# W1 loaded into the memory of W2 and of hT's second buffer, with a new list of orders and engines

## The chip, the cores and the metric

The kernel runs on one core of a Trainium2 chip. The time is device microseconds of one execution, from the first to the last instruction with what the launch adds around them; the median of three runs of the kernel before is 260.54 us (260.16 to 260.61). Engines are named as in the profile: PE (TensorE, matmul), DVE (VectorE), ACT (ScalarE), POOL (GpSimd) and SP (SyncE, which only issues transfers).

## The reference

Nyström attention on q, k and v of shape 8 x 8 x 576 x 64 (batch, heads, sequence, head size), then a feed-forward block on the result, seen as 8 x 576 x 512:

```python
q_lm, k_lm = means of q and k over 32 segments of 18 rows
A, Bm, C = sm(q, k_lm), sm(q_lm, k_lm), sm(q_lm, k)
Z = Bm.T / (norm1(Bm) * norminf(Bm) + 1e-6)
for _ in range(6):
    Z = 2 * Z - Z @ Bm @ Z
x = A @ Z @ C @ v                       # heads put side by side: 576 x 512 per batch
xn = (x - mean(x)) / sqrt(var(x) + 1e-6) * g_ln
out = x + relu(xn @ w_ch1) @ w_ch2      # 512 -> 2048 -> 512
```

## The kernel before, in words

The work is cut into 1571 named operations, each with the engines that may do it and the buffers it uses. A list at the top of the file (`ORDER`, lines 19 to 105) gives the order in which they are emitted and the engine of each, so `28G` is operation 28 on POOL, `95S` operation 95 issued by SP. Every engine works off its own operations strictly in that order; where one waits, all behind it on that engine wait too. A buffer's slot is given out at its first use and comes back after its last, in the order of the list.

Eight batches are computed. Batch 0 is prepared alone, batch 1 alone, then 2 and 3, 4 and 5, 6 and 7 in pairs. For a batch, the stages are:

- loads of q, k and v. For batch 0 SP loads fp32 into the staging buffers `stg` (six slots), and an operation `cast_...` turns each into fp16 (`nat_q`, `nat_k`, `natv`). For the other batches POOL loads q and k with the conversion in the transfer, and SP loads v into two buffers `vs`.
- for batch 0: transposes on PE (`turns_k0` and so on), their copies (`turned_...`, to `xT_k`, `xT_q`), segment sums (`sums_...`), `klm` and `qbd`, then `psb_0`, `expb_0`, `softmax_0` (line 366), `gram_a_0`, `gram_b_0`, `scaled_0` and six iterations `step_0_i` (PE) and `next_0_i` (DVE, line 425), then `product_0` with v, `rcv_0`, `cv_00`, `cv_01`, `zt`, `zc`, and the copies `ztc`, `zsum`, `zcbd`. `ea` holds the exponentials of A; `ln`, `inv` (ACT) and `norm` normalize it.
- `rows` and `x`: the attention's output in blocks of 128 rows, `measure` its mean and variance.
- `psm_bf`, `m16_bf`: W1 multiplied by the batch's small matrix, in four quarters f of 512 columns; for batches 0 and 1 the column mean of W1 (`less_f`, from `less_mean_fc` on PE) is added in `m16`.
- `psh`, `relu`: the hidden rows, 16 chunks of 128 for a batch, evicted by ACT or DVE into `hT` (two buffers, `hT0` and `hT1`, by the batch's parity).
- `pso`, or from batch 2 on a scheme with seven products of halves (`ps7a`, `ps7c`, `ps7e`, with sums `mix` of quarters of W2), then `done`/`add7` into x and the stores.

Weights: g is loaded as `g_rows`, turned by PE (`turn_g`) and written to `g_sb` by DVE. W1 (512 x 2048, fp32, 4 MB) comes in eight pieces of 512 KB, `load_w1_i`, piece i holding quarter f = i // 2 and half of the 512 rows. In the kernel before each goes into a slot of `stg`, which q, k and v of batch 0 have used first, so the load waits for a cast to free one. Two operations `scale_w1_ic` per piece multiply by g and write fp16 to `w1_16` (line 357 on POOL and DVE, line 203 on ACT). W2 is loaded by POOL in four pieces with conversion into `w2_16`.

`warm_i` are matmuls on zeros, 24 of 160 columns in one and four of 128 in each of 14 others, which stand in PE's order while the first data come in.

In the kernel before, SP's order begins k01, k00, q00, q01, v00, v01, g, then W1's pieces 2, 3, 1, 0, 4, 5, 6, v10, piece 7, v11. POOL's begins with the constants, `cast_k01`, `load_q10`, `load_k10`, `cast_v00`, the first scalings.

Of the kernel before, what the change touches and what calls it, by code (L numbers as in the profile page):

```python
# [16 lines left out]
P = 128  # L17

ORDER = """
0G 20P 23P 4S 12P 14P 24P 17P 11P 2S 1S 3S 6S 7S 10P 21P 28G 38P 25A 26D 34P 39D 40P 29P 30A 31P 27D  # L20
37P 32P 42D 41D 18P 33D 43P 65P 44A 45D 66A 61P 67P 46P 47P 250G 48D 22P 19P 15P 62A 68A 69A 71D
245G 49P 50D 63P 35P 13P 79G 80D 51P 52D 64A 36A 81P 70D 53P 72P 73A 5S 95S 54D 8P 9D 105A 106G 55P
56D 57P 74P 82D 260P 83D 58D 16P 84D 96S 59P 75A 76A 60D 85P 251D 86D 89P 90D 87P 88D 126P 261A 262D
108G 77G 94S 103G 93S 97S 101G 91D 92D 78D 107A 102G 127P 128P 129P 130A 167P 141P 142A 252P 253A
145P 169D 104A 168D 98S 254D 149P 150D 147P 148A 172P 173A 176P 247P 177A 248A 259D 255D 174P 175A
246D 256P 257A 146A 170P 171D 109G 110G 121P 122P 123P 111G 124P 268P 156P 258D 151D 249D 267P 112A
125A 275A 269A 270A 271A 157D 277A 158D 131P 132P 133P 134P 178P 163P 278D 279D 117G 273A 433G 274A
99S 113G 135A 180D 263S 164A 159P 280P 281D 160A 165P 166A 114G 264A 100S 115G 116G 265S 118G 136P
137P 266G 161P 179D 429G 119G 138P 139P 162D 282P 283D 140A 181P 182A 183P 284P 276D 285A 143P 187P
184D 286P 144A 188A 272D 152D 185P 186A 287D 297P 298D 299D 189P 191D 190D 288P 289A 294P 290P 295A  # L30
201P 202P 296A 300P 301A 291D 292P 293A 120G 455G 212P 213P 435G 436G 437G 310P 438G 445G 302A 303G
308P 309A 214P 330P 434D 444D 312D 311D 313D 332D 192P 193A 153D 154D 198P 199A 155A 441D 430D 439D
431D 331D 442D 440D 432D 443D 234P 556D 215P 304P 235P 236P 305A 306A 196P 446G 447G 203P 204P 194P
195A 237P 238P 205P 206P 451G 197A 307G 314P 315A 337P 339P 448G 449D 822G 338A 555D 239P 240P 241P
322P 207P 208P 574D 565D 569G 450D 340A 323A 216P 242D 209D 210S 217P 324D 341P 343D 223P 335P 244S
336A 342D 333P 463D 218P 219P 577G 452D 220D 344P 352P 353D 467G 468G 469G 470G 334A 826G 348P 345A
349A 346P 347A 457G 318P 319A 224P 316P 317A 225P 226P 227P 481P 458G 465D 459G 460G 482A 350P 454D
354D 357P 471D 464D 472D 351A 453D 363P 228P 229P 364D 358A 361P 230P 362A 461D 462D 365D 493P 494A
359P 368P 360A 483P 495P 355P 325D 326D 505A 369A 356A 231D 233A 200G 374P 375P 366P 367A 370P 371A
573G 506D 456D 507P 508P 509D 320P 321D 385P 484P 486A 487A 489A 510P 834D 511D 466D 491A 386P 387P  # L40
485A 388P 211S 512P 376P 473S 474G 490A 377P 496P 498A 501A 499A 497A 513D 514P 327D 488D 492D 328D
396P 397P 475S 476G 566G 828G 829G 830G 831G 572G 477S 478G 838G 839G 844G 564G 568G 503A 378P 379P
380P 515D 823D 502A 221S 504D 372P 516P 479S 480A 500D 517D 836D 528P 529P 530D 531D 398P 399P 373A
381P 522P 518P 389P 329A 866S 382D 418P 519D 824D 559D 520P 521D 523A 532P 419P 420P 524A 533A 534A
558D 550P 551D 552D 553D 548P 549A 421P 422P 423P 536P 424P 425P 848G 535G 832D 833D 554D 232S 867A
537A 538A 539G 560D 525P 527A 400P 401P 557D 426D 427S 605P 526A 606A 840G 841G 594P 595A 561D 540P
541A 390P 391P 611P 612A 837D 596D 827D 392P 393D 825D 850G 851G 852G 563D 603P 604A 853G 562D 859D
842D 860G 861G 843D 579P 613P 614A 407P 580A 601P 602A 609P 610A 1217G 585P 408P 845D 599P 409P 607P
600A 410P 411P 586A 597P 608A 542A 543G 856D 615P 598A 576G 626P 616A 412P 413P 581P 627A 402P 862G
394S 582A 570G 567D 617D 589D 835D 863G 858D 590D 618P 619A 634P 635A 643P 583P 584A 620P 621A 624P  # L50
414P 571G 874P 625A 622P 623A 628P 629A 644P 544P 847D 857D 545A 846D 591D 546A 875D 403P 632P 872S
633A 645P 630P 647P 592D 631A 646P 415D 877P 648P 649P 650P 864D 865D 854D 404D 855D 1191G 886P 638D
637G 641G 663P 664P 665P 639D 640D 662G 428S 417S 406S 661D 593A 882A 884A 879A 880A 883A 652D 878A
651D 657D 887A 889P 892A 896A 658D 666P 668D 894A 895A 849D 667D 653P 654P 711P 722P 712A 723A 891A
890A 655P 656P 547G 575G 675P 676P 677P 728P 729A 678P 695P 696A 1192D 713D 716P 881D 1194D 717A
724P 725A 876P 888P 1213G 660D 587P 870S 714P 416S 659D 871G 873G 384S 1229G 642G 1230G 1231G 726P
898A 715A 679D 682D 669P 897D 727A 588A 730P 222S 1232G 899D 900P 901P 731A 718P 732P 902D 743P 719D
578G 903P 904D 670P 720P 734A 733A 721D 744A 671P 672P 673D 699P 700A 893D 739P 636G 1203D 1239S
701P 905P 243S 741P 906D 740A 751P 674D 742A 703P 752A 907P 735P 736A 737P 383S 868S 681S 680S 683S
738A 702D 908D 909P 1219G 1195G 1220G 1221G 685P 704D 697P 698A 915P 917A 916A 910D 911P 1222G 759P  # L60
760P 749P 811P 925P 750A 761P 885D 869G 921P 926A 927A 753G 922P 1225D 755G 912D 913P 705D 706D 745P
# [1202 lines left out]
```

## Time and profile before

| | |
|---|---|
| runs | 260.16, 260.54, 260.61 us |
| profiled execution, span from first to last instruction | 258.5 us (2.0 below the median of the runs; its own time with the launch is not recorded) |
| PE busy | 249.9 us, 97% |
| DVE busy | 212.3 us, 82% |
| ACT busy | 163.9 us, 63% |
| POOL busy | 177.5 us, 69% |
| granted TensorE clock | 1.00 throughout |
| moved by DMA | 36.32 MB |

In the profile the first number of a row of a timeline is its start and the second its length, in us from the start of the span; "x8" counts the instructions put together, and the part in brackets is the time that the engine stood idle before it and what ended it. "PE busy" counts a matmul to its modelled end and so overstates how full PE is where matmuls are few. In the chain of waits each piece was released by the one before it. In the rows by stretch, the columns are the stretch, its length, the busy time of PE, weight loads, DVE, ACT and POOL with counts, the granted clock, the DMA share and GB/s. A line number is often that of a helper (L193 matmul, L200 copy, L203 ACT's function, L207 two-tensor operation, L210 scalar-tensor-tensor), so rows are told apart by the tiles.

### The profile page before, as it was taken

To read this page: it belongs to the slowest core of one execution; us is meant where nothing else is said; L and a number is where in the kernel's file an instruction comes from. 1 tells how busy PE (TensorE), PEld (TensorE's weight loads), DVE (VectorE), ACT (ScalarE), POOL (GpSimd) and SP (SyncE) were. 2 spreads that over 40 slices of the span, in tenths; PEclk is the share of its full clock that TensorE was granted. 3 is DMA by queue.
4 is the path that set the end of the run, shared out by engine and by line. 5 is a ranking of instruction groups with operands and counts; after the bars stand their busy time and mean duration, and the time that the engine had idled before them with its cause. 6 is when DMAs were issued, how large, how long until landed. Compare 5 with 4: busy or idle time off the path is not lost.

```text
span 258.5 us, 8351 instructions
## 1 busy us (share of the span) xinstructions
PE 249.9 (97%) x3499; PEld 179.8 (70%) x3499; DVE 212.3 (82%) x472; ACT 163.9 (63%) x304; POOL 177.5 (69%) x180
## 2 busy tenths in 40 slices
PE   7898999999999999999999999999999999999993
PEld 7766465556554557777766787777867787788981
DVE  1669899999999989997998869898547999878661
ACT  1588886747766999778756997868666245644000
POOL 8324899689794789699999995782078505966600
PEclk9999999999999999999999999999999999999999
DMA  6999999999749176949704832500130100510356
GB/s 234 367 269 338 374 210 208 207 235 244 227 127 178 29 164 87 221 89 286 140 4 121 231 93 61 127 3 3 41 85 0 44 20 9 115 23 20 82 121 184
DMA packets 23277, 36.32 MB, mean 140 GB/s; under 512 B 2116, under 2 KB 11592, under 8 KB 23240
## 3 DMA queue, kind: packets, MB, share of 16 engines
q1 hardware_dynamic: 12456, 23.37, 29.6%
q0 software_dynamic: 9504, 10.36, 25.1%
q10 hardware_dynamic: 1280, 2.07, 3.1%
q8 instruction: 27, 0.44, 0.7%
q14 instruction: 10, 0.08, 0.1%
HBM read 36.70 MB, written 9.44 MB: 178 GB/s over the span
## 4 chain that ended last, share of the span: by engine, by line
PE 85%; DMA 7%; ACT 3%; DVE 2%; issue 1%; SPq 1%; ACTq 0%; DVEq 0%
PE psh L193 23%; PE ps7a L193 16%; PE pso L193 15%; PE ps7c L193 8%; DMA w1s<-in_moe_w_ch_dram 5%; PE ps7e L193 4%; PE psm L193 3%; PE psy L193 3%; DMA stg_q<-in_q_dram 3%; PE it L193 2%; PE pscv L193 2%; PE psd L193 1%; PE psec L193 1%; PE psea L193 1%; PE pso_74a L193 1%
## 5 line engine op out<-in xcount | busy, mean ns | idle before, releaser
L203 ACT ACTIVATE hT<-psh 128x576 f16<-128x576 f32 x106 | 65.8, 650 | 30.4 <-PE psh L193 28.6
L193 PEld LDWEIGHTS <-hT 128*128 128x128 f16 x688 | 64.6, 98 | 22.6 <-issue 3.1
L193 PE MATMUL psh<-ea,m 128*128 128x288 f16 x512 | 78.2, 286 | 0.1
L193 PEld LDWEIGHTS <-m 128*128 128x128 f16 x512 | 48.9, 98 | 15.6 <-issue 1.3
L193 PE MATMUL pso<-w,hT 128*128 128x512 f16 x176 | 45.5, 380 | 0.0
L207 POOL TENSOR_TENSOR mix<-hT 128x1024 f16<-128x1024 f16 x8 | 17.0, 2125 | 27.4 <-ACT hT L203 27.4
L210 DVE SCALAR_TENSOR_TENSOR x<-ps7a,rstd,x 128x256 f32<-128x256 f32 x48 | 21.3, 477 | 6.7 <-PE ps7a L193 4.9
L193 PE MATMUL ps7a<-mix,hT 128*128 128x256 f16 x192 | 25.9, 273 | 0.0
L1068 DVE TENSOR_SCALAR hT<-psh 128x576 f16<-128x576 f32 x22 | 16.4, 753 | 10.1 <-PE psh L193 9.9
L997 DVE BATCH_NORM_STATS2 six<-x 128x6 f32<-128x512 f32 x36 | 24.2, 673 | 0.0
L207 POOL TENSOR_TENSOR ea<-ea,lns 128x576 f16<-128x576 f16 (+1 forms) x14 | 17.7, 1261 | 7.2 <-ACT lns L203 4.0
L200 ACT CAST m<-psm 128x512 f16<-128x512 f32 (+1 forms) x25 | 19.1, 793 | 4.5 <-PE psm L193 3.4
L200 ACT COPY x<-psy 128x512 f32<-128x512 f32 (+1 forms) x29 | 16.8, 587 | 7.6 <-PE psy L193 7.2
L193 PEld LDWEIGHTS <-mix 128*128 128x128 f16 x192 | 18.2, 98 | 4.3 <-issue 1.5
L207 POOL TENSOR_TENSOR mix<-mix,hT 128x1024 f16<-128x1024 f16 x8 | 16.9, 2124 | 6.2 <-DVE mix L207 5.8
L207 POOL TENSOR_TENSOR hT<-hT 128x1024 f16<-128x1024 f16 x9 | 19.1, 2123 | 0.2
L207 POOL TENSOR_TENSOR hT<-hT,mix 128x1024 f16<-128x1024 f16 x7 | 15.1, 2166 | 4.4 <-PE ps7e L193 2.5
L214 DVE TENSOR_REDUCE part<-xT_k 128x32 f16<-128x576 f16 x24 | 17.1, 737 | 0.0
L207 POOL TENSOR_TENSOR asum_q<-asum_q 128x256 f32<-128x256 f32 (+1 forms) x24 | 15.1, 628 | 1.5
L203 ACT ACTIVATE ec<-psec 128x256 f16<-128x256 f32 (+1 forms) x42 | 12.4, 428 | 5.3 <-PE psec L193 5.3
L193 PE MATMUL psy<-zcbd,ea 128*128 128x256 f16 x80 | 14.8, 273 | 0.2 <-ACT x L200 0.2
L200 POOL CAST natv<-stg_v 128x1152 f16<-128x1152 f32 (+1 forms) x12 | 13.8, 1163 | 1.4 <-DMA stg_v<-in_v_dram 1.3
(174 smaller groups left out, 471.2 us busy)
## 6 DMA issues: line engine op xcount, KB each, us to landing
out_dram<-x SPq DMA_DIRECT2D x55, 128.0 KB, 2.7
stg_v<-in_v_dram SPq DMA_DIRECT2D x10, 576.0 KB, 5.1
w1s<-in_moe_w_ch_dram SPq DMA_DIRECT2D x8, 512.0 KB, 11.6
nat_q<-in_q_dram POOLq DMA_DIRECT2D x7, 576.0 KB, 8.7
nat_k<-in_k_dram POOLq DMA_DIRECT2D x7, 576.0 KB, 7.5
w<-in_moe_w_ch_dram POOLq DMA_DIRECT2D x4, 512.0 KB, 8.5
out_dram<-x ACTq DMA_DIRECT2D x15, 128.0 KB, 2.4
stg_v<-in_v_dram SPq DMA_DIRECT2D x6, 288.0 KB, 4.5
```

The lines of the kernel that those rows point to most:

```text
L193: keep(nc.tensor.matmul(o, l, r, start=start, stop=stop, tile_position=(rb, cb), skip_group_check=(skip or cb != 0)))
L200: keep(nc.scalar.copy(o, i) if e == "A" else ENGINES[e].tensor_copy(out=o, in_=i))
L203: keep(nc.scalar.activation(*args, **kw))
L207: keep(ENGINES[e].tensor_tensor(out=o, in0=a, in1=b, op=f))
L210: keep(ENGINES[e].scalar_tensor_tensor(out=o, in0=a, scalar=s, in1=b, op0=f0, op1=f1))
L214: keep(nc.vector.tensor_reduce(out=o, in_=i, axis=axis, op=f))
L997: keep(nc.vector.bn_stats(out=T(f"six_{j}")[:], in_=T(f"x_{j}")[:]))
L1068: keep(nc.vector.tensor_scalar(out=o, in0=T(psh)[:, :, 0:HS], scalar1=0.0, scalar2=None, op0=ALU.max))
```

## The change

W1's pieces get no buffers of their own. Pieces 0 to 3 are loaded into the memory of `w2_16` (a quarter each, seen as fp32), pieces 4 to 7 into the second buffer of `hT`, which is then taken from the start of the program. A W1 load needs no staging slot any more. A load of W2 now has to wait until the scalings that read the W1 piece in the same quarter are done, and the first writes to the second hT buffer until the scalings of pieces 4 to 7 are.

```diff
     def def_weights():
+        if hT(1) not in kinds:
+            buf(hT(1), "hT1", [P, MCH, S + 64], FP16)
+
+        def place_of(i):
+            f, half = divmod(i, 2)
+            if f < 2:
+                return w2_16[:, ts(i, 4), :].rearrange("p m d -> p (m d)").bitcast(FP32).rearrange(
+                    "p (c d) -> p c d", c=2)
+            return T(hT(1))[:].rearrange("p m t -> p (m t)")[:, ts(i - 4, 4 * DM)].bitcast(FP32).rearrange(
+                "p (c d) -> p c d", c=2)
+
+        def held(i):
+            return () if i < 4 else (hT(1),)
+
         for i in range(8):
-            n = f"w1s_{i}"
-            buf(n, "stg", [P, 2, DM], FP32)
             f, half = divmod(i, 2)
-            op(f"load_w1_{i}", "S", (n,),
-               lambda e, n=n, f=f, half=half: dma(
-                   e, T(n)[:], w1_src[:, 2 * half:2 * half + 2, ts(f, DM)]))
+            op(f"load_w1_{i}", "S", held(i),
+               lambda e, i=i, f=f, half=half: dma(e, place_of(i), w1_src[:, 2 * half:2 * half + 2, ts(f, DM)]))
...
-                def scale(e, n=n, f=f, c=c, kk=kk):
-                    o, src = w1_16[:, kk, ts(f, DM)], T(n)[:, c, :]
+                def scale(e, i=i, f=f, c=c, kk=kk):
+                    o, src = w1_16[:, kk, ts(f, DM)], place_of(i)[:, c, :]
...
-                op(f"scale_w1_{i}{c}", "GAD", (n,), scale)
+                op(f"scale_w1_{i}{c}", "GAD", held(i), scale)
```

The list of orders is new for its first 727 operations, up to the middle of the preparation of batches 4 and 5; the other 844 are the same. The operations and their numbers are the same, and 46 of them change their engine. What the new list does, by engine, where it differs early:

- SP: k00, k01, q00, g, q01, v01, W1's pieces 2, then v00, then pieces 3, 0, 4, 1, 5, 6, v11, 7, v10.
- PE: twelve `warm` operations (before: nine) stand ahead of the first transposes, the other three between `turns_k0` and `turns_k1` (before: six spread to the end of the iterations). `turn_g` follows `turns_k1`. `product_0` stands behind `step_0_4`, the first two `less_mean` of quarter 1 ahead of it; `product_10` of batch 1 and its last steps stand behind the first `pso` of batch 0.
- DVE: `cast_k00`, `turned_k0`, `cast_q00`, `turned_k1`, `turned_q0`, `qbd`, `turned_q1`, `softmax_0`, `scaled_0`, `g`, then the iterations with `cast_v00` behind the fourth. New on DVE are `cast_q00`, `turned_q0`, `turned_q1` (from ACT), `cast_v00` and `scale_w1_10` (from POOL), `norm_10_0` (from POOL); gone from it are `cast_q01`, `klm`, three `relu` of batch 0 and three `next_1_i` (to ACT), three `norm` of batch 0 and `cast_v01` (to POOL).
- ACT: `cast_q01`, `klm`, `expb_0`, and so on; it scales parts of pieces 2, 3, 0, 5 and 7 (before 2, 3, 1 and 5), with `less_0` ahead of its scaling of piece 5 (before: behind it); `cast_v10` goes to POOL.
- POOL: the constants, `load_q10`, `cast_k01`, `cast_v01`, `load_k10`, four `norm` of batch 0 among the scalings; `load_w2_0` behind the scaling of piece 5, then `load_w2_1` and `load_q20` behind those of pieces 6 and 7 (before: `load_w2_0`, `load_q20`, those scalings, `load_w2_1`).

```diff
-0G 20P 23P 4S 12P 14P 24P 17P 11P 2S 1S 3S 6S 7S 10P 21P 28G 38P 25A 26D 34P 39D 40P 29P 30A 31P 27D
...
+2S 0G 24P 22P 19P 17P 250G 4S 16P 20P 21P 15P 14P 10P 28G 1S 26D 5S 3S 18P 23P 32P 27A 33D 7S 13P
...
```

165 lines of the change are left out of this document (82 added, 83 removed).

## The prediction

> **What bounds the kernel now.** I read the page first, then the chain of waits, the DMA view of the first 35 us, the busy time by stretch, and last the timeline of the start, row by row. The page and two of the stretches:
>
> ```profile
> span 258.5 us, 8351 instructions
> PE 85%; DMA 7%; ACT 3%; DVE 2%; issue 1%; SPq 1%; ACTq 0%; DVEq 0%
> 24.00:30.00 6.00, 5.71 (x96) 3.47 (x93) 5.01 (x11) 5.01 (x15) 4.82 (x7) 1.00 1.05 396
> 40.00:50.00 10.00, 10.00 (x90) 5.48 (x89) 9.84 (x21) 6.62 (x15) 8.76 (x12) 1.00 1.23 208
> ```
>
> From about 40 us on TensorE (the first column after the length) has no gap left, and the chain that ended last is 85% TensorE. The matmuls are the same before and after, so the end moves by what the change does to the moment at which TensorE is full, and by little else. The rest of the chain lies in the first 40 us; these are its pieces that matter:
>
> ```profile
> 15.84 11.95 DMA w1s<-in_moe_w_ch_dram
> 27.81 0.73 ACT w L203
> 28.89 0.12 ACT less L200
> 29.04 1.42 DVE m L210 x2
> 30.91 0.61 PE psh L193 x4
> ...
> 36.51 0.56 ACT hT L203
> ...
> 37.12 0.75 PE pscv L193 x34
> ...
> 38.28 0.44 DVE cv L207
> 39.53 0.86 PE pso L193 x4
> ```
>
> The sixth piece of W1 is issued at 15.84, lands 11.95 us later, ScalarE scales it at 27.81, and only then comes the column mean (less) of the first quarter of W1, the m tiles and at 30.91 the hidden rows. It looks as if W1 were late because it waited for staging buffers. The DMA view of the first 35 us (40 slices of 0.875 us) says otherwise:
>
> ```profile
> GB/s 0 0 84 276 398 408 400 411 406 392 398 390 359 283 292 249 231 257 279 290 281 302 266 276 280 300 377 406 421 389 377 404 398 390 389 367 273 222 215 202
> w1s<-in_moe_w_ch_dram SPq DMA_DIRECT2D x8, 512.0 KB, 11.6
> ```
>
> ```profile
> 6.12 1.37 POOL L223 DMA_DIRECT2D nat_q<-in_q_dram  x1
> ```
>
> From 3.5 us there is no hole. Where the figure falls to 231 to 302 the loads issued by POOL are in flight, which turn fp32 into fp16 on the way and are counted by the smaller side. A 512 KB piece at 400 GB/s is 1.3 us of transfer, and takes 11.6 us to land: it stands in a queue behind others. The W1 pieces were waiting in the DMA queue, not for its doors.
>
> **The change, part by part.** *The loads of W1.* The eight issues stay on SP, lose their wait for a freed staging buffer, and so enter the queue up to 10 us earlier. They cost nothing more, and gain nothing in sum, since the engines that carry them are full. What counts is the order of the bytes. Before: k, q, v of batch 0, then pieces 2, 3, 1, 0, 4, 5, 6, v, 7, v. After: v01 ahead of piece 2, v00 behind it, then 3, 0, 4, 1, 5, 6, v, 7, v. So piece 5 is still the sixth (lands at 27.8 as now), piece 1, which the first quarter needs, falls from third to fifth place (two pieces, 2.6 us), and v00 lands after piece 2 and not before it. POOL issues its load of q of batch 1 (now at 6.12) ahead of its first cast; if that brings its bytes forward by its own 1.4 us, SP's queue loses half of the bandwidth for as long, and piece 3 lands up to 1.4 us later. Bounds for piece 3: 0 and +1.4; I take +0.7.
>
> *The start.* These rows carry the first chain:
>
> ```profile
> 1.40 6.26 PE L193 MATMUL idle<-zeros 128*128 128x128 f16 x56 [1.40 <-DVE zeros L252]
> 13.11 0.84 PE L193 MATMUL idle<-zeros 128*128 128x128 f16 x12
> 8.20 0.76 DVE L200 COPY xT_k<-pst_k 128x1152 f16<-128x1152 f16 x1 [1.03 <-PE pst_k L197]
> 9.42 0.76 DVE L200 CAST nat_q<-stg_q 128x1152 f16<-128x1152 f32 x1 [0.47 <-DMA stg_q<-in_q_dram]
> 10.79 0.42 DVE L207 TENSOR_TENSOR qbd<-pss_q,mask 128x256 f16<-128x256 f32 x1 [0.41 <-PE pss_q L193]
> 11.89 0.21 DVE L214 TENSOR_REDUCE rsum<-it 128x2 f32<-128x64 f32 x1
> 13.70 0.22 DVE L207 TENSOR_TENSOR st<-it,cinv 128x64 f16<-128x64 f32 x1
> 17.48 0.29 DVE L210 SCALAR_TENSOR_TENSOR st<-st,it 128x128 f16<-128x128 f16 x1
> 18.21 0.28 DVE L210 SCALAR_TENSOR_TENSOR st<-st,it 128x128 f16<-128x128 f16 x1
> 18.41 0.41 DVE L633 TENSOR_SCALAR cv<-pscv,rcv,cinv 128x130 f16<-128x130 f32 x1
> 18.82 0.39 PE L193 MATMUL idle<-zeros 128*128 128x128 f16 x4
> 20.36 0.27 DVE L214 TENSOR_REDUCE zsum<-pszc 128x2 f32<-128x128 f32 x1
> 20.84 0.72 DVE L207 TENSOR_TENSOR zcbd<-pszc,heads 128x256 f16<-128x256 f32 x2
> 20.41 0.74 POOL L207 TENSOR_TENSOR ea<-ea,lns 128x288 f16<-128x288 f16 x1
> ```
>
> Today 9 warm-up groups stand ahead of the first transposes (56 matmuls, to 7.66); after, 12 (68). At the later rate (12 in 0.84) the other 12 add 0.84 less overlap, so the transposes of k start at about 8.2. Then VectorE has, one behind the other, the copy of k's transposes, the cast of q00 (ScalarE did it), the other copy of k and the copy of q (ScalarE's too): four of 0.76 from 8.9, so 11.95, and qbd ends at 12.4 where it ended at 11.2. Another copy of 0.76 now stands between qbd and the softmax, which starts at 13.1, not 11.89. From there to the scaled st takes 2.0 us as now (11.89 to 13.92), so 15.2. Six iterations at 0.73 (17.48 to 18.21) are 4.4, and the cast of v00 (0.76, which waits for that later landing) and small pieces stand among them in VectorE's queue: 0.6 more is my estimate, and two cv of 0.41 stand behind them. That gives the last cv at about 21.1, against 18.8 now. Of these 2.3 us not all count, because cv is not what ends last now; the rows of the first quarter to be multiplied are:
>
> ```profile
> 21.32 0.59 ACT L200 CAST less<-psf 128x512 f16<-128x512 f32 x1 [0.68 <-PE psf L193]
> 21.96 1.41 DVE L210 SCALAR_TENSOR_TENSOR m<-less,zsum,psm 128x512 f16<-128x512 f16 x2
> 23.48 1.14 PE L193 MATMUL psh<-ea,m 128*128 128x288 f16 x8
> ```
>
> The first m tile waits for less (ready at 21.9), and W1's path is the later one. After, cv at 21.1 is followed by a quarter of a us of matmul and four small pieces of VectorE (zcbd twice 0.36, zsum 0.27, and a copy of about as much, 1.3 together with the hand-overs), so the first m starts at about 22.8, not 21.96, and the first hidden rows at 24.3, not 23.48. The norms that went from VectorE to POOL (0.74 each, two behind the second logarithm) end at 23.2 by the same walk and fit under that. **Term A: +0.9 us**; bounds +0.2 (the copies overlap better, piece 3 as early as now) and +1.6 (piece 3 late by 1.4).
>
> *The first quarter, ScalarE's load.* ScalarE takes over three hidden-row evictions from VectorE, more scalings, and gives up v's cast:
>
> ```profile
> 24.17 1.19 ACT L203 ACTIVATE hT<-psh 128x576 f16<-128x576 f32 x2
> 27.81 0.72 ACT L203 ACTIVATE w<-w1s,g_sb 128x512 f16<-128x512 f32 x1 [0.86 <-DMA w1s<-in_moe_w_ch_dram]
> 33.47 1.16 ACT L200 CAST natv<-stg_v 128x1152 f16<-128x1152 f32 x1
> 30.00:40.00 10.00, 9.67 (x145) 6.21 (x145) 9.63 (x26) 8.20 (x17) 9.18 (x13) 1.00 1.19 240
> ```
>
> From its first less to its second it has twelve pieces (both less, four evictions and four x of 0.6, one scaling of 0.72, one small copy): from 22.2 some 7.0 us, and half a us of waits for the rows between, so the second less ends near 29.7, where it ended at 29.0. The good side is in the same place: the scaling of piece 5, which held ScalarE 0.86 us until 27.81, now stands behind that less. VectorE gets a scaling of piece 1 in its queue (0.4, estimated from the 0.76 for a cast 1152 wide), with the m tiles queued behind it; piece 1 lands near 26.5 (1.3 before piece 5), before they could run. So the m tiles of this quarter are late by 0.7 (less) to 1.5 (VectorE waits for the small copy of k's sums that ScalarE does just before); I take 1.1, which is 0.2 beyond A. **Term B: +0.2**, bounds -0.6 (less at 28.4, ScalarE kept free) and +0.8.
>
> *From 30 to 45 us.* ScalarE does three more evictions (0.6 each), two more scalings net, two more copies of the iteration (0.42 is what one costs now, an estimate here), and one cast of v less (1.16): net 2 us, against 1.8 us that it is idle between 30 and 40. Some 0.3 of it comes through to TensorE, which has two PSUM buffers for the hidden rows and waits for their eviction. Against that stands a gain: batch 1's product is put behind parts of batch 0's second layer, so the stretch from 37.12 to 39.53, where the chain goes through VectorE (0.44 and smaller) behind an eviction of 0.56, is covered: -0.6. **Term C: -0.3**, bounds -0.9 and +0.8.
>
> *W2 and q of batch 2.* The four W2 loads on POOL must now wait for W1's scalings out of the same memory:
>
> ```profile
> 28.51 0.81 POOL L223 DMA_DIRECT2D w<-in_moe_w_ch_dram  x1
> 29.32 0.75 POOL L223 DMA_DIRECT2D nat_q<-in_q_dram  x1
> 39.56 1.16 POOL L207 TENSOR_TENSOR asum_q<-nat_q 128x512 f32<-128x512 f16 x1
> ```
>
> The first W2 load goes from 28.51 to about 29.3, q of batch 2 from 29.32 to about 33.5 (behind two more scalings of pieces that land at 29 and 32 and the second W2 load), what is behind it on POOL are v's casts and the sums at 39.56. The first second-layer matmuls stand at 39.53, so W2 has 10 us; the sums of q slip by about 1.5 us and feed batch 2, whose hidden rows come after all of batch 1's. Taken at 0; without that cover each would cost its slip. hT's second buffer is written by batch 1's hidden rows, which both lists put well behind the last scaling. Engine swaps behind 45 us (x, mix, one norm, three casts of v) move VectorE's and ScalarE's loads by less than 1 us each way. **Term D: 0**, bounds -1.0 and +0.8. The order is the same from batch 3's middle on, so a lag at 100 us passes to the end through a full TensorE.
>
> Sum: 0.9 + 0.2 - 0.3 + 0 = +0.8 on the span of 258.5, so 259.3. The median of the runs shown, 260.54, stands 2.0 above that span; with the same 2.0 the forecast is 261.3 us.
>
> [...]
>
> **The rivals.** *Early W1* (the change does what it says): W1 is never waited for. For it speaks the 11.95 us piece in the chain, against it the slices without a hole. TensorE's gaps between 24 and 40 (0.29 and 0.33) and the 1.9 us that the chain spends in scale, less and m after the landing would go: -2.5, 258.0 us. *Faster, by ScalarE's queue*: the start loses little, and the second less, no longer behind the wait of 0.86, comes at 28.4; with A at its lower bound and B and C at theirs, 0.2 - 0.6 - 0.9 = -1.3, 259.2 us. It decides when the first hidden rows come before 24.0. *No change*: A's lag is refilled, since TensorE waited until 30.91 anyway: 260.5. *Slower through the clock*: the change takes the fillers that stood between 10 and 19 us to the front, ahead of 9.5. The first 56 matmuls took 6.26 us where the rate of the 12 gives 3.9, so one more cold stretch costs up to 2.3 us: 263.6. Against it, the four fillers at 18.82, after a thin stretch, still took 0.39. [...]
>
> **How the numbers follow.** A measurement of this kernel tells some 0.2% (0.5 us) from no change. Chances: my forecast (slower, +0.5 to +2.0) 0.41, clock 0.04, no change 0.21, faster by ScalarE 0.28, early W1 0.06. So faster 0.34, same 0.21, slower 0.45. The range takes in the faster rival with its own error and A, B and C at their upper bounds: 258.6 to 263.0; the forecast's own is 261.0 to 262.5.
>
> **What would show it.** Right: DMA slices again without a hole from 4 to 30 us, W1's time to landing longer than 11.6 while its scalings stand where they stand now; first transposes past 8; softmax at 13; first hidden rows at 24 or later; ScalarE without gaps from 22 to 38; no wait for W2. Wrong: hidden rows of the first quarter before 30.0, scalings before 17, or TensorE with fewer gaps past 45 us, where I counted nothing.

## The result, and the profile after

The changed kernel takes 263.21 us (median of 5 runs, 261.32 to 264.97), the kernel before 260.54 (260.16 to 260.68): a ratio of 1.0103, 95% interval 1.0064 to 1.0142. It is slower, as forecast, but by 2.7 us and not by 0.8, and the median stands 0.2 us above the range. Ratios, here and below, are taken from undisturbed runs alone and so differ a little from the quotient of the medians. The spans of the two profiled executions differ by 3.0 us and not by 2.7: every run takes 1.7 to 1.8 us longer than its span, so the execution of the kernel before that was profiled, with a span of 258.5, was some 0.3 us faster than the median.

The runs differ far more than those of the kernel before, and the fastest, at a granted clock of 1.000, took 261.32 us; the others had 0.998, 0.993, 0.992 and 0.981 and took 262.95 to 264.97. Lines of the page of the profiled execution (263.21 us):

```profile
span 261.5 us, 8340 instructions
...
PEclk9997999999999999999999999999999999999999
...
q8 instruction: 27, 0.44, 0.7%
...
PE 88%; DMA 6%; SPq 1%; ACT 1%; issue 1%; DVE 1%; POOL 0%; POOLq 0%
...
w<-in_moe_w_ch_dram SPq DMA_DIRECT2D x4, 512.0 KB, 15.5
hT<-in_moe_w_ch_dram SPq DMA_DIRECT2D x4, 512.0 KB, 14.5
```

The pieces of W1 are issued earlier and take 15 us to land where they took 11.6. The 7 in the clock's row is new, at 19.6 to 26.1 us. The DMA view of the first 35 us of the changed kernel has no hole from 3 us on:

```profile
GB/s 0 0 147 408 408 379 226 354 340 351 403 330 284 284 254 260 282 288 360 412 400 307 263 279 283 280 281 353 401 403 389 412 395 395 389 382 202 205 211 167
```

The timeline of its start:

```profile
7.90 0.67 PE L197 MATMUL pst_k<-ident,nat_k 128*128 128x128 f16 x9
...
11.90 0.42 DVE L207 TENSOR_TENSOR qbd<-pss_q,mask 128x256 f16<-128x256 f32 x1
...
13.04 0.23 DVE L214 TENSOR_REDUCE rsum<-it 128x2 f32<-128x64 f32 x1
...
20.21 0.72 DVE L643 TENSOR_SCALAR cv<-pscv,rcv,cinv 128x130 f16<-128x130 f32 x2
20.59 0.69 POOL L367 TENSOR_SCALAR w<-w,g_sb 128x512 f16<-128x512 f32 x1 [3.00 <-DMA w<-in_moe_w_ch_dram]
21.33 0.59 PE L193 MATMUL psf<-w,lesser 128*128 128x512 f16 x2 [1.35 <-POOL w L367]
...
23.49 1.41 DVE L210 SCALAR_TENSOR_TENSOR m<-less,zsum,psm 128x512 f16<-128x512 f16 x2
25.10 2.02 PE L193 MATMUL psh<-ea,m 128*128 128x288 f16 x8
...
30.22 0.58 ACT L200 CAST less<-psf 128x512 f16<-128x512 f32 x1
```

The chain stands where it was put, within 0.3 us, down to the last cv at 20.9. Then the third product for less waits until 21.33 for piece 3 of W1, and the first hidden rows take 2.02 us where the same eight took 1.14. By stretch (columns as before; the clock stands ahead of the last two):

```profile
20.00:21.00 1.00, 0.00 (x0) 0.00 (x0) 0.93 (x5) 0.56 (x1) 0.41 (x1) 1.00 1.13 278
21.00:22.00 1.00, 0.67 (x26) 0.25 (x25) 0.00 (x0) 0.73 (x2) 0.46 (x2) 1.00 1.13 281
22.00:23.00 1.00, 0.58 (x32) 0.22 (x14) 0.73 (x3) 0.70 (x2) 1.00 (x2) 1.00 1.14 281
23.00:24.00 1.00, 1.00 (x11) 0.42 (x5) 0.86 (x3) 0.35 (x1) 0.81 (x2) 0.73 1.11 293
24.00:25.00 1.00, 0.75 (x5) 0.51 (x4) 0.90 (x2) 1.00 (x3) 0.12 (x1) 0.50 1.07 391
25.00:26.00 1.00, 1.00 (x6) 0.62 (x5) 0.66 (x2) 0.33 (x1) 0.00 (x0) 0.50 1.08 409
26.00:27.00 1.00, 1.00 (x7) 0.63 (x5) 0.97 (x4) 0.65 (x1) 0.25 (x1) 0.56 1.03 388
27.00:28.00 1.00, 1.00 (x9) 0.67 (x8) 1.00 (x3) 0.82 (x2) 1.00 (x2) 1.00 1.06 410
```

Behind thin work from 20 to 23 us the granted clock is 0.50 for 3.4 us (0.54 of the stretch from 23, two whole ones, 0.88 of the one from 26).

To see where time is lost for good I compare when TensorE has done the same amount of matmul work (columns times share of the array, summed in order, without the fillers) in two traces, and call the difference the lag behind the kernel before. It is 2.5 us at 25 us, 1.3 on average from 45 to 77, and then jumps to 2.98, where it stays to the end: the spans differ by 3.0. So what the halved clock cost was mostly absorbed, and 1.7 of the 3.0 us are lost behind 77 us, in a place that the prediction did not look at. TensorE's timeline of the changed kernel there:

```profile
79.11 0.45 PE L193 MATMUL psea<-xT_q,lm 32*32 32x288 f16 x22
80.63 0.32 PE L193 MATMUL psea<-xT_q,lm 32*32 32x288 f16 x8 [1.07 <-issue]
```

In the middle of 32 equal small multiplications TensorE issues nothing from 79.28 to 80.63 us, and waits for no semaphore ("issue"). The page's row `q8 instruction` (the kernel before has the same) is the only lead: 27 transfers, 0.44 MB, and in the trace's packets 16,384 bytes each. The trace has 7009 multiplications, weight loads and waits of TensorE, 260 for each transfer. Counted in the trace, the last instruction ahead of the gap is number 2241 = 8 x 256 + 193. The DMA view from 78.15 to 79.10 us holds the eighth such transfer (78.19 to 79.07 in the trace's packets):

```profile
q0 software_dynamic: 116, 0.13, 82.9%
q1 hardware_dynamic: 49, 0.10, 27.5%
q8 instruction: 1, 0.02, 5.8%
```

My theory from here on, *instructions*: TensorE's program comes in blocks, one to a transfer, and while TensorE works through one the next is transferred. A block is taken as 256 instructions, an estimate from the 260 counted for each transfer and from the stops seen in the runs below, behind numbers 705, 2241 and 3777, which lie 1536, six times 256, apart. Where data loads are in flight, that transfer begins late (3.48 us after the block was entered here, 0.60 in the kernel before), and a block that is worked off too fast ends before the next is there. The block of instructions 1986 to 2241 took 5.90 us in the kernel before; the new list packs more small multiplications into it, 4.57 us of work. The rivals: *clock* (the fillers that were moved ahead of 9.5 us make the clock fall, and that is the loss), and that psea waits for data or a buffer.

### The profile page after: what moved, and what is told of

Its sections match the earlier page's. It is cut to its first block, busy times and chain, and to the rows that moved or that the text cites. A ratio compares the mean times of both kernels' runs of the same rounds, so it can differ in the third digit from the quotient of the medians.

```text
span 261.5 us, 8340 instructions
## 1 busy us (share of the span) xinstructions
PE 251.3 (96%) x3499; PEld 180.0 (69%) x3499; DVE 209.8 (80%) x468; ACT 165.1 (63%) x308; POOL 178.3 (68%) x180
## 4 chain that ended last, share of the span: by engine, by line
PE 88%; DMA 6%; SPq 1%; ACT 1%; issue 1%; DVE 1%; POOL 0%; POOLq 0%
PE psh L193 25%; PE ps7a L193 16%; PE pso L193 15%; PE ps7c L193 8%; DMA w<-in_moe_w_ch_dram 6%; PE ps7e L193 4%; PE psm L193 4%; PE psy L193 3%; PE it L193 3%; PE psec L193 2%; PE pscv L193 2%; PE psd L193 1%; SPq L223 1%; PE psea L193 1%; PE psf L193 1%; PE pso_74a L193 1%
## 5 line engine op out<-in xcount | busy, mean ns | idle before, releaser
L203 ACT ACTIVATE hT<-psh 128x576 f16<-128x576 f32 x109 | 68.8, 657 | 29.8 <-PE psh L193 27.7
L193 PE MATMUL psh<-ea,m 128*128 128x288 f16 x512 | 79.6, 289 | 0.0
L193 PEld LDWEIGHTS <-m 128*128 128x128 f16 x512 | 49.1, 98 | 16.6 <-issue 2.2
L207 POOL TENSOR_TENSOR ea<-ea,lns 128x576 f16<-128x576 f16 (+1 forms) x16 | 18.5, 1161 | 8.7 <-ACT lns L203 8.7
L1078 DVE TENSOR_SCALAR hT<-psh 128x576 f16<-128x576 f32 x19 | 14.1, 753 | 9.7 <-PE psh L193 9.5
L207 POOL TENSOR_TENSOR asum_q<-asum_q 128x256 f32<-128x256 f32 (+1 forms) x24 | 15.9, 664 | 1.5
L193 PE MATMUL psy<-zcbd,ea 128*128 128x256 f16 x80 | 15.4, 283 | 0.2 <-DVE m L210 0.2
L207 POOL TENSOR_TENSOR asum_q<-nat_q 128x512 f32<-128x512 f16 x12 | 13.9, 1155 | 1.3 <-DMA nat_q<-in_q_dram 0.9
```

What stands on the lines that cost most here:

```text
L193: keep(nc.tensor.matmul(o, l, r, start=start, stop=stop, tile_position=(rb, cb), skip_group_check=(skip or cb != 0)))
L203: keep(nc.scalar.activation(*args, **kw))
L207: keep(ENGINES[e].tensor_tensor(out=o, in0=a, in1=b, op=f))
L1078: keep(nc.vector.tensor_scalar(out=o, in0=T(psh)[:, :, 0:HS], scalar1=0.0, scalar2=None, op0=ALU.max))
```

## The experiments

**1. Fillers back, memory alone, fillers away, a load later.** Four kernels on one chip.

`e1_fillers_back`, TensorE's order:

```diff
-24P 22P 19P 17P 16P 20P 21P 15P ... 18P 23P 32P ... 13P 11P 12P 38P
+24P 17P 20P 21P ... 23P 32P ... 11P 12P 38P ... (warm_8 behind sums_q0; warm_12, 9, 5 behind psb_0; warm_3 behind psc_0; warm_6 behind step_0_5)
```

> The changed kernel with six of its 14 filler groups (28 idle multiplications of TensorE, which write a tile that nobody reads) put back where the kernel before has them, between 11 and 20 us. Clock theory: the changed kernel's runs have granted clocks of 0.981 to 1.000 and their times follow them, since TensorE stands idle between the steps of the chain without the fillers; here the clock is 1.000 in all runs, the slice at 19.6 us shows 9, the spread falls under 0.7 us and the median to that of the run with clock 1.000, 261.3 us. Instruction theory (TensorE stood 1.35 us at 79.3 us because its next block of instructions had not come): that stall stays, and the median is 262.3 to 263.2 us. Start theory (the fillers lie on the chain): 0.3 us slower than the changed kernel.

Measured: 263.08 us, ratio 1.0082 (1.0062 to 1.0102); the groups hold 24 multiplications, not the 28 of that text. Its clock row and TensorE at 80 us:

```profile
PEclk9988999999999999999999999999999999999999
```

```profile
80.20 0.32 PE L193 MATMUL psea<-xT_q,lm 32*32 32x288 f16 x8 [0.96 <-issue]
```

The clock falls all the same, now to 0.50 from 17.6 us, behind another thin stretch (TensorE busy for 0.56 us from 16 to 17 and 0.61 from 17 to 18), and the mean clock is under 0.996 in 4 of 6 runs. The places with which the profile of the old list stood at 1.00 throughout do not hold the new one there, so this says nothing yet on the clock's price. The stall is there again, behind instruction 2241 (lag 1.2 before it, 2.6 after).

`e2_memory_only`: the old list with the new `def_weights`.

> The kernel before with W1 loaded into the memory of W2 and of the second hT, and its old list of orders and engines. The forecast's theory (the DMA slices are full, so memory that is free earlier brings nothing): 260.5 us within 0.5. Rival, early W1: pieces of W1 that no longer wait for a staging buffer land earlier and the first quarter starts sooner: 259.5 us or less. Rival, W2 and hT wait: load of W2 or the first hidden rows of the second buffer come after the last scaling of W1: over 261 us.

Measured: 260.76 us, ratio 1.0007 (0.9995 to 1.0020): the same. Its DMA view and TensorE's third product for less:

```profile
w<-in_moe_w_ch_dram SPq DMA_DIRECT2D x4, 512.0 KB, 16.6
```

```profile
22.21 0.59 PE L193 MATMUL psf<-w,lesser 128*128 128x512 f16 x2 [1.57 <-ACT w L203]
```

Issued up to 4.8 us earlier (11.07 us for 15.84, the sixth), the pieces stand as much longer in the queue (16.6 and 16.2 us to landing, median, for 11.6). In this execution one even came later, so that the product stands at 22.21 where the kernel before has it at 20.70, and TensorE is 1.0 us behind from there to the end; the median of the 12 runs shows nothing of it. So the memory alone brings no gain and no loss that these runs can tell, 0.5 us being the upper end of the interval.

`e3_before_no_mid_fillers`: the old kernel, `warm_8, 12, 9, 5, 3, 6` moved to the front.

> The kernel before with its six filler groups between 11 and 19 us moved to the front, as the changed kernel has them, and nothing else changed. Clock theory: granted clock under 0.998 in most runs, times spread over 1 us or more, median 0.5 to 3 us above the kernel before. Rival (the fillers are not needed, and lie on the chain with 0.39 us here and there): clock 1.000, 260.1 to 260.6 us.

Measured: 260.78 us, ratio 1.0023 (1.0000 to 1.0046). The median does not move, but 3 of 11 runs have clocks of 0.980 to 0.984 and take 262.2 to 263.2 us, which no run of the kernel before does (its clocks in all the experiments are 0.989 to 1.000). Even the profiled run shows a dip to 0.50, from 14.7 to 18 us, and loses only 0.6 by it:

```profile
PEclk9979999999999999999999999999999999999998
```

So without the fillers in these places the clock fell lower in three runs than in any run with them, and what their lack cost was now nothing, now 1.5 to 2.5 us.

`e4_late_v40`, SP's order:

```diff
- ... load_v40 store_5_0 load_v51 ...
+ ... store_5_0 load_v40 load_v51 ...
```

> The changed kernel with one load of v (576 KB, issued at 73.8 us, first read at some 105 us) issued after the store at 92 us. Instruction theory: the DMA engines have room when TensorE's block of instructions is asked for at 74.7 us, the fetch that began 3.5 us later and ended at 79.1 us comes sooner, the stall of 1.35 us at 79.3 us is gone or under 0.3 us, TensorE's lag behind the kernel before is near 1.2 us at 90 us in place of 3.0, and the median is 1.3 to 1.8 us lower, 261.4 to 261.9 us, with the spread by clock as it was. Clock theory alone: 263.2 us, as before this edit. Rival: the stall is a wait for data of the loads: it stays where it is, or v comes late at 105 us and the time rises.

Measured: 262.22 us, ratio 1.0040 (1.0021 to 1.0058). The fetch began 2.4 us after the block was entered and not 3.5, the gap behind instruction 2241 is 0.26 us, the lag goes from 1.1 to 1.6:

```profile
78.80 0.75 PE L193 MATMUL psea<-xT_q,lm 32*32 32x288 f16 x30
```

As the instruction theory has it. The median is 0.3 us above what it was to be, but three of the eight runs took 265.2 to 265.3 us; the median of the other five is 261.77, inside the forecast. Clocks of 0.984 to 0.993 stand in 6 of the 8.

**2. Work moved, idle stretches filled.**

`e5_psea_later`, TensorE's order:

```diff
- ... psea_10 step_2_3 pso_12_06 pso_14_00 psd_20 ...
+ ... pso_12_06 pso_14_00 psea_10 step_2_3 psd_20 ...
```

> The changed kernel with TensorE's order alone edited: the 32 small multiplications of psea that stood 1.35 us at 79.3 us, and the step behind them, are moved behind two output tiles (four long multiplications, 0.87 us). Instruction theory: the block of 256 instructions that ran out at 79.28 us now lasts 0.87 us longer and the next block still comes at some 80.6 us, so the stall is 0.3 to 0.6 us in place of 1.35 and the median falls by 0.7 to 1.0 us, to 262.3 us or so. Rival, the stall is a wait of psea for its data or for a buffer: psea's later place changes nothing of when it starts behind the stall (80.6 us), or the stall goes wholly. Clock theory alone: 263.2 us.

Measured: 264.19 us, ratio 1.0115 (1.0072 to 1.0157). A miss. The block now lasted 6.0 us and nothing stands behind instruction 2241, but the time came back at once:

```profile
81.74 0.59 PE L193 MATMUL pso<-w,hT 128*128 128x512 f16 x2 [0.49 <-DVE x L210]
82.26 0.50 PE L193 MATMUL psea<-xT_q,lm 32*32 32x288 f16 x32
...
83.58 0.40 PE L193 MATMUL psd<-ea,bones 128*128 128x288 f16 x2 [0.62 <-ACT ea L203]
```

The output tiles wait for VectorE to empty their buffers, and what follows psea waits for ScalarE's exponential of it, late by as much. The lag jumps by 1.7 as in the changed kernel. The order cannot be mended by pushing psea back. (The profiled run lost another 1.4 us at 34.3 us, where TensorE waited for VectorE's bmD.)

`e6_v40_and_fillers` and `e7_fillers_in_holes`: `warm_9, 12` behind `step_0_2`, `warm_6, 3, 5` behind `step_0_5`, `warm_8` behind `zt_00`; e6 with the load of e4 as well.

> The changed kernel with the late load of v of e4_late_v40 and, beside it, six filler groups (24 multiplications) moved from the front into the two stretches where TensorE stands idle in all profiles of the changed list: two groups at 16.6 us, three at 19.9, one at 21.9. Clock theory: the clock falls to 0.50 for some 3.5 us wherever a stretch of little work lies ahead of it (16 to 18 us and 20 to 21.3 us), and with both stretches filled it stays at 1.00: all runs at 0.996 or above, spread under 1 us, median 261.0 to 261.4 us, which is what the forecast without clock and stall gave. Rival, the clock's fall has nothing to do with these stretches: clocks of 0.98 to 0.99 remain and the median stays at 262.2 us as in e4_late_v40.

> The changed kernel with the same six filler groups moved into the two idle stretches at 16.6 and 19.9 to 21.9 us, and the load of v where the change has it. If clock and instruction block are two separate causes: clock 0.996 or above, spread under 1 us, the stall of 1.2 to 1.4 us at 79 us stays, median 262.3 to 262.9 us. If the low clock at 24 us were what shifts the later work into the stall: no stall, 261.3 us.

Measured: e6 262.28 us, 1.0054 (1.0029 to 1.0078); e7 262.64 us, 1.0076 (1.0042 to 1.0110). The clock row of e7 (e6 has the same):

```profile
PEclk9999999999999999999999999999999999999999
```

19 of these 20 runs have clocks of 0.996 or more, where the changed kernel had 2 of 5: with the two thin stretches filled the clock hardly fell. But the median is lower by 0.6 to 0.9 us only, within the intervals, the runs still spread over 3.1 us (e6) and 5.1 us (e7) where under 1 was expected, and the stall is in both profiles. TensorE in e7:

```profile
24.28 1.26 PE L193 MATMUL psh<-ea,m 128*128 128x288 f16 x8
...
78.89 0.32 PE L193 MATMUL psea<-xT_q,lm 32*32 32x288 f16 x8 [0.85 <-issue]
```

The load of v moved in e6 did not help there: the fetch began 3.4 us after the block was entered, the two loads of POOL at 70.5 and 75.2 us being in flight. So one load of three is not the cause alone, and e4 presumably had luck with the place of the others: POOL's second load was issued 0.5 us ahead of the block there, and 0.4 us behind its start in e6.

**3. The same order, other block limits.**

`e8_shift_112` (the changed kernel) and `e9_before_shift` (the kernel before):

```diff
-    warm(24, 160)
-        warm(4, 128)
+    warm(24, 128)     # e8; unchanged in e9
+        warm(8, 32)   # e8; warm(2, 256) in e9
```

> The changed kernel, its order untouched, with 56 more idle multiplications in the filler groups (14 groups of 8 narrow ones in place of 4 wide, about the same time): TensorE's program is 112 instructions longer ahead of the work, so each 256-instruction block ends 112 instructions earlier in the work. Instruction theory: counted on the trace, the blocks around the stall then last 4.3 us from 71.4 and 5.8 to 6.7 us from 76, in place of 4.6 us from 74.7 where 5.9 were needed, so the stall at 79 us goes (no gap over 0.5 us without a releaser between 70 and 90 us), the lag does not jump there, and the median is 1.0 to 1.8 us lower, 261.5 to 262.2 us. Rival, psea waits for its data, a buffer or the loads: the stall stays at psea, 263.2 us. The clock and the arrival of W1 stay as they were and keep the spread.

> The kernel before, its order and memory untouched, with 28 idle multiplications fewer (14 filler groups of 2 wide ones in place of 4, the same time): 56 instructions fewer, so its blocks end 56 instructions later in the work, and one of them would then last only 3.5 us, from 75.4 to 78.9 us, with a load of v in flight. Instruction theory: a stall of 0.3 to 1.8 us without a releaser appears near 79 us, where the kernel before has none, the lag against it jumps there by as much, and the median is 260.9 to 262.4 us. Rival (the stall belongs to the new order's data or buffers): no stall, 260.5 us within 0.4.

> The changed kernel with both causes taken away: the six filler groups in the two idle stretches as in e7_fillers_in_holes, and the program 112 instructions longer as in e8_shift_112. If low clock and instruction block are the whole of the loss beyond the start: clock 0.996 or above, no stall at 79 us, median 260.3 to 261.4 us (the lag of e7_fillers_in_holes before its stall was -0.1 to 0.2 us in its profile, the forecast's terms gave +0.8), spread by the arrival of W1 of 1 to 2 us. Rival, something else in the new order costs as well: 261.8 us or more with neither low clock nor stall.

Measured: e8 264.69 us, 1.0144 (1.0103 to 1.0185); e9 262.12 us, 1.0063 (1.0039 to 1.0087); e10 (e7 with e8's fillers) 263.24 us, 1.0095 (1.0079 to 1.0112). TensorE in e8, where the gap left psea and stands in the products ahead of it:

```profile
78.04 0.37 PE L193 MATMUL pscv<-natv,ecT 64*64 64x130 f16 x12 [1.31 <-issue]
```

In e10:

```profile
78.58 0.36 PE L193 MATMUL pscv<-natv,ecT 64*64 64x130 f16 x11 [1.45 <-issue]
```

And in e9, the old list, where the kernel before runs through all 72 of these products from 129.34 us on:

```profile
129.65 0.95 PE L193 MATMUL pscv<-natv,ecT 64*64 64x130 f16 x49
131.23 0.54 PE L193 MATMUL pscv<-natv,ecT 64*64 64x130 f16 x23 [0.63 <-issue]
```

In e8 and e10 the gap is behind instruction 2241 of the new count, which is 112 instructions earlier in the work; in e9 behind 3777 = 14 x 256 + 193. With no data, buffer or order touched, the gap moves with the count: the rival, a wait of psea, falls. In all 16 traces TensorE stops for over 0.6 us without a semaphore eleven times, each time behind an instruction whose number leaves 193 when divided by 256; e10 has a second stop of the kind, 0.7 us behind number 705, at 19.8 us, and having kept its stall it tests neither outcome of its text. What I had expected wrongly is that a shift would take it away. Every cut of that stretch of the new list into 256 leaves a block of 4.9 us or less, and in e9 the block that I had named (75.7 to 79.0 us, 3.4 us long) passed unharmed because its transfer began 0.26 us after it was entered, while another ran dry, 50 us later: that its time lies in the forecast is luck. e8's median is not the price of the stall alone, since five of its six runs had clocks of 0.974 to 0.993. All the same, 28 idle multiplications fewer cost the kernel before 0.6%.

**4. Without the loads.**

`e11_loads_out`, GpSimd's order, with SP's of e4:

```diff
- ... mix_06 load_q50 ... asum_q403 load_k40 ... asum_q413 asum_q500 asum_q501 norm_20_0 norm_21_0 load_k50 ...
+ ... mix_06 load_k40 ... asum_q403 ... asum_q413 load_q50 norm_20_0 norm_21_0 load_k50 asum_q500 asum_q501 ...
```

`e12_holes_again` is the list of e7 once more, on the same chip, to compare with.

> The kernel of e7_fillers_in_holes with the loads taken out of the stretch around 75 us: of the two loads that GpSimd issues at 69.8 (q of pair 5) and 74.6 us (k of pair 4), the k is issued at 69.8 and the q behind the sums at some 78 us, with its own first sums behind the next load of k, and SyncE's load of v that follows at 73.8 us is issued after the store at 92 us. TensorE's instructions are the same and in the same order. Instruction theory: TensorE asks for the block behind its 2241st instruction at 73 to 75 us, and its fetch now begins within 2.4 us in place of 3.5, so no stall or one under 0.3 us stands behind the 2241st instruction, the lag does not jump at 79 us, and the median is 0.8 to 1.4 us under that of e12_holes_again on the same chip. Rival (the fetch is late whatever the loads do, or the stall is not the loads' work): a stall of 1.0 to 1.4 us as before, no change of the median.

> The kernel of e7_fillers_in_holes again, on the chip of e11_loads_out. Instruction theory: a stall of 0.9 to 1.4 us behind the 2241st instruction again, since what is ahead of it is the same. Theory on the arrival of W1: the lag behind the kernel before at 60 us is set by when the second piece of W1 lands (-0.1 us where it was scaled from 20.1 us on, 1.2 us from 20.6 us, 1.7 us from 22.1 us), and differs from the other profile of this kernel as that time does. Median 262.3 to 262.9 us, clocks of 0.996 or above in nearly all runs.

Measured: e11 261.57 us, 1.0049 (1.0023 to 1.0076); e12 262.73 us, 1.0072 (1.0048 to 1.0096). TensorE in e11, then in e12:

```profile
79.77 0.32 PE L193 MATMUL psea<-xT_q,lm 32*32 32x288 f16 x8 [0.65 <-issue]
```

```profile
80.63 0.32 PE L193 MATMUL psea<-xT_q,lm 32*32 32x288 f16 x8 [1.35 <-issue]
```

The median falls by 1.2 us, with intervals that overlap, but the stall is only shortened, 0.93 us against 1.63, since the transfer still began 3.2 us after the block was entered (3.8 in e12) and not within 2.4. So in the kernel of e7 POOL's two loads were left out, and v's was issued behind the store, `e13_no_loads`:

```diff
+                if w % 2 == 0 and (nm, units[w][0]) in (("q", 5), ("k", 4)):
+                    op(f"load_{nm}{units[w][0]}0", "G", (), lambda e: None)
...
-                n = f"nat_{nm}{units[w][0]}"
+                n = f"nat_{nm}{({('q', 5): 4, ('k', 4): 3}).get((nm, units[w][0]), units[w][0])}"
```

> The kernel of e7_fillers_in_holes without the two loads that GpSimd issues at 69.8 and 74.6 us: it leaves out q of batch 5 and k of batch 4 and computes with q of batch 4 and k of batch 3 in their place, and SyncE's load of v at 73.8 us comes after the store at 92 us. TensorE's instructions are the same in number and order. Theory, the loads make the fetch late: between 73 and 79 us the DMA engines have next to nothing, the fetch asked for at 74.4 us begins within 1.2 us, no stall of over 0.1 us stands behind the 2241st instruction, TensorE's lag behind the kernel before stays after 79 us what it was ahead of it, and the median is 1.0 to 1.6 us under the 262.7 us of e7_fillers_in_holes and e12_holes_again: 261.1 to 261.7 us. Rival, the fetch is late by itself where the block is dense: the stall stays at 1.0 us or more. Rival, the work behind waits for something else as well: the stall goes and waits of its size come in its place, as in e5_psea_later.

Measured: 261.60 us, 1.0047 (1.0030 to 1.0064), all runs from 260.96 to 262.33. TensorE, and the DMA view from 73.8 to 78.3 us:

```profile
78.21 0.50 PE L193 MATMUL psea<-xT_q,lm 32*32 32x288 f16 x32
```

```profile
DMA packets 1, 0.02 MB, mean 4 GB/s; under 512 B 0, under 2 KB 0, under 8 KB 0
...
q8 instruction: 1, 0.02, 1.5%
```

The block is as dense as ever, 4.51 us, and there is no gap. The eighth transfer begins 0.78 us after the block is entered. That settles it for this block: without the loads in flight the transfer began after 0.78 us, with them after 2.4 to 3.8, and it is the loads that made TensorE's instructions late. The kernel before agrees: the DMA engines moved 4 GB/s when it entered this block, and its transfer began after 0.60 us. The time does not settle it: 261.60 us lies in the forecast, but on a chip where the kernel before took 260.33, and as a ratio it is 0.3% under e7, with intervals that overlap. Side by side, block 1986 to 2241:

| kernel | entered | transfer begins, after | ends | work | gap |
|---|---|---|---|---|---|
| before | 72.71 | 73.31, 0.60 | 74.36 | 5.90 | 0 |
| changed | 74.71 | 78.19, 3.48 | 79.07 | 4.57 | 1.35 |
| e4 | 74.40 | 76.80, 2.40 | 77.73 | 4.57 | 0.26 |
| e7 | 73.17 | 76.67, 3.49 | 77.64 | 4.58 | 1.14 |
| e8 | 72.29 | 75.80, 3.51 | 76.77 | 4.22 | 1.53 |
| e5 | 76.33 | 79.19, 2.86 | 80.07 | 6.00 | 0 |
| e13 | 73.80 | 74.58, 0.78 | 75.68 | 4.51 | 0 |

The lag of e13 is 0.5 us from 45 to 77 and 0.85 to the end; its span, 259.3 us, is the one that was forecast, by coincidence, since it lacks two loads and has its fillers elsewhere.

`e14_q10_later`, in the kernel of e7:

```diff
- 0G 250G 28G ...     (constants, load_q10, cast_k01)
+ 0G 28G 250G ...
```

> The kernel of e7_fillers_in_holes with GpSimd's load of q of batch 1 behind its cast of k01 again, as in the kernel before (issued some 1.1 us later). Theory, the bytes of that load ahead of W1's second piece make W1 late: the first quarter of DMA traffic keeps its full rate 1 us longer, and the scaling of that piece on GpSimd begins by 20.1 us in place of the 20.1 to 22.1 us that the profiles of the new list show; the lag at 60 us is 0.3 us or less, and the median 0.4 to 1.0 us lower than 262.7 us. Rival: the arrival of W1 varies from run to run whatever this load does, or TensorE waits for that q itself (17 us) instead: median within 0.4 us of 262.7.

Measured: 266.16 us, 1.0246 (1.0215 to 1.0278). A miss by 4 us, and 3 us above the rival as well, which had named the wait but no price for it:

```profile
19.25 1.12 PE L193 MATMUL psl_q<-nat_q,pairs 128*128 128x128 f16 x9 [2.23 <-DMA nat_q<-in_q_dram]
```

In the new list the sums of that q stand in TensorE's queue ahead of `step_0_3`, so the whole chain waits 2.23 us, and the clock falls behind the hole (six runs of 0.984 to 0.991). Piece 3 of W1 is scaled from 20.20 us on, no sooner than in the best profiles of e7's list, so this load does not explain its arrival.

The new list with the old staging buffers was not tried: W1's pieces would stand in it ahead of the casts that free their slots.

## Why the prediction was right about the start and wrong in its time

**W1's loads.** Right, though the pieces entered the queue only 0.7 to 4.2 us earlier, place by place, and not up to 10: SyncE's issues themselves now take up to 3.2 us, where they took 0.4 to 0.8. Full queues, pieces that land later after their issue by as much as they are issued earlier, piece 3 scaled at 20.59 where +0.7 on 19.75 was taken; *early W1* falls with e2. That SP's queue loses half of its bandwidth to POOL's loads is what the kernel before shows: 402 GB/s alone from 5 to 9 us, and 180 (0.54 MB in 3 us) from 16 to 19 with POOL's loads in flight. Piece 3 is also what varies: it is scaled from 20.14 us in e7, 20.46 in e13, 20.96 in e12, 21.49 in e11, 22.09 in e6, and the lags from 45 to 77 us are -0.1, 0.5, 1.0, 1.0 and 1.7 in the same order. All five have one order up to 69 us.

**A, +0.9.** Right step by step down to the last cv: transposes 7.90 (8.2 forecast), qbd's end 12.3 (12.4), softmax 13.04 (13.1), last cv 20.9 (21.1). Behind it, A came out at its upper bound, +1.6: the first m started at 23.49 for 22.8, the first hidden rows at 25.10 for 24.3. The small matmuls that follow cv stand in TensorE's queue behind the third product for less, and so waited for piece 3 until 21.33, which the walk from cv to m left out. In e7, where piece 3 came 0.45 us sooner and the clock stayed up, m started at 23.05 and the rows at 24.28; of the 0.8 us between the two kernels about half is piece 3, and the rest the halved clock (four psy took 1.01 us for 0.60).

**B, +0.2, and C, -0.3.** C's sum is misadded: 1.8 + 1.44 + 0.84 - 1.16 are 2.9 us more work for ScalarE, not 2; measured, it was busy for 9.28 us from 30 to 40, for 8.20 before. The second less ended at 30.8 behind the halved clock and at 29.25 in e7; 29.7 was forecast, 29.0 is the kernel before. What is left of A to C at 45 us is -0.1 to 1.7 us, with 0.5 to 1.3 in the changed kernel, e12 and e13, where +0.8 was forecast. The terms' sum was right within its bounds; that their size depends on when a piece of W1 lands was named, that it changes from run to run was not. Two of the signs named were missed: the transposes started just ahead of 8, and ScalarE had gaps between 22 and 38 us (13.70 of 16 us busy, 13.90 before).

**D, 0 behind 45 us.** This is the step that failed. It asked which engine's load moves, found less than a us each way, and stopped there, because TensorE had no gap left. It did not count TensorE's instructions, nor what the loads do to their arrival, and TensorE did get a gap. The changed kernel's profile lost 1.35 us to the missing block and some 0.4 to the new order behind 77 us (e13 has that 0.4 without the stall). 1.26 + 0.38 + 1.35 is 2.99, the difference of the spans; so D measured +1.7 where its bounds were -1.0 and +0.8, and A to C +1.26 for +0.8. W2's and q's loads themselves went where the step put them: 29.64 (29.3) and 33.61 (33.5), and nothing waited for W2.

**The clock.** The rival with a chance of 0.04 came true as an event: the clock falls behind the thin stretches in most runs of every kernel with the new list and no fillers in them. Its price did not show in this profile (in three runs of e3 it was 1.5 to 2.5 us): the lag of 2.5 us is down to 1.0 at 40 us, most of it refilled before the second layer. Between e7 and the changed kernel stand 0.6 us of median, which the intervals do not resolve. The row against it, four fillers at 18.82 that still took 0.39, was no evidence: those fillers stood in the list and were themselves among those without which, in e3, three runs had clocks of 0.980 to 0.984. The clock was halved for 3.4 us in this profile, and as long in those of e1, e3 and e4. TensorE was not idle ahead of that: in the 3.41 us before the fall (20.06 to 23.47 us) it was busy for 1.72. And the clock does not fall each time: in the profile of e2, idle from 20.6 to 22.2 us, it stayed at 1.00. In the clock's records of the changed kernel and the kernel before, every change stands a whole multiple of 3.41 us behind the first record: 5 and 6 times at 23.47 and 26.88 us, and 75 and 74 times just behind the ends of the two spans. What decides whether it falls was not tested.

**What stays open.** How much of the median's 2.7 us each cause takes: the stall is shown in the profiles, where it varies from 0.85 to 1.67 us, and not run by run, and the intervals of e7, e12 and e13 overlap. Single runs of 264 to 266 us at clocks of 0.997 and more (e6, e7, e11, e12) were not profiled; what they lose, and where, is not known. Why piece 3 lands up to 2 us apart is not known either.

## What to carry to other kernels

Here the instructions of a long program, 7009 counted on TensorE, were themselves a load: count them, mark each 256th (here from number 193 on), and look for blocks that are short and begin while data are being loaded, since there the new order cost a stall (1.35 us in the changed kernel) that no wait in the code shows. A row with "issue" as its releaser in the middle of equal instructions was the sign, and a few idle instructions more or fewer, which moved the limits and nothing else, were the test. And before fillers are called useless, take them away in an experiment and look at the spread of the runs, not at one median.

## What was not expected of the hardware

- Instructions came by DMA while the kernel ran: 27 transfers of 16,384 bytes in the two profiles of before and after, from 12.82 to 246.08 us in the kernel before. With the DMA engines nearly empty (4 GB/s) the transfer for the block at 73 to 75 us began 0.6 (kernel before) and 0.8 us (e13) after the block was entered; with loads in flight (299 GB/s from 74.7 to 78.15 us in the changed kernel) it began 2.4 to 3.8 us after, in the kernels with the new list. It took 0.9 to 1.1 us, and where TensorE had run dry it went on 1.25 to 1.6 us after its end. In the kernels that stopped there with the loads in flight, 5.5 to 6.2 us passed from one block's start to the next (4.8 in e4), where the work in the block took 4.2 to 4.6.
- The clock fell to 0.50 with TensorE at work: in the changed kernel it came behind 20 to 23 us with TensorE busy for 0.00, 0.67 and 0.58 us of the three.
- VectorE's product for bmD took 1.96 us in e5 (from 33.76), while POOL issued a load (33.60) and cast v (34.39 to 35.56), where it takes 0.29 in the kernel before and 0.45 in the changed one. No run here separates what POOL did there from chance.
